# Linear attention and a GELU layer on one core: a warm-up in five fp32 matmuls, warm matmuls between the first kv and x steps, and first touches spread over rows

## The chip, the cores and the metric

The kernel runs on one core of a Trainium2 chip. The metric is the device time of one execution in microseconds. A program on one core has no second die to compare with, but each execution lists the mean clock that TensorE was granted.

## The reference, cut to what matters

```python
q_s = softmax of q over the 64 features          # batch 8, heads 8, sequence 576
k_s = softmax of k over the sequence
kv  = einsum('bhsd,bhse->bhde', k_s, v)
x   = einsum('bhsd,bhde->bhse', q_s, kv)          # as 4608 tokens x 512
out = gelu(x @ w_in) @ w_out                      # 512 -> 2048 -> 512, fp32 in and out
```

(The original spells the softmaxes out, and GELU with erf.)

## The kernel before: the parts that the change and the argument touch

TensorE works in bf16. For each batch: transposes of q, kv products, x products, then the h stage (64 matmuls of 128x512 for `x @ w_in`) and the y stage (64 for `@ w_out`). Batch 0 has no earlier batch to hide behind, so its front waits for the loads, and 27 matmuls on zeros, the warm-up, fill TensorE meanwhile (in before's trace their weight loads start 0.43 us apart until 4.07 us; at the full clock that the trace records from 3.98 on, a matmul of this shape takes 0.216, 64 of them 13.81).

```python
zeros = singles.tile([128, 512], BF16)

def warm(n):
    ps = psum_y.tile([128, DM], FP32, tag="y")
    for i in range(n):
        nc.tensor.matmul(ps, zeros[:, 0:128], zeros, start=True, stop=True)

touch = singles.tile([16, 4, 2], FP32)           # four tiny reads on another queue
for i, a in enumerate((k[0, 0, 0:16, 0:2], v[0, 0, 0:16, 0:2],
                       moe_w_in[0:16, 0:2], moe_w_out[0:16, 0:2])):
    nc.scalar.dma_start(out=touch[:, i, :], in_=a)

load_main(0, "q", q, 2); load_pair(0, "k", k, 2); load_pair(0, "v", v, 4)
wi = [load_wi(i) for i in range(5)]              # w_in in blocks of 256, 256, 512, 512, 512 columns
wo = [load_wo(i) for i in range(3)]              # ... batch 1, the last of w_out, batch 2
nc.vector.memset(zeros, 0.0)
setup_tiles()                                    # three more VectorE memsets
warm(27)
...
tp_mm(0, 0)                                      # transposes
warm(2)
...
tp_mm(0, 1)
kv_mm(0, 0); kv_norm(0, 0, 1); tp_evac(0, 1)     # kv, its normalisation on VectorE
x_mm(0, 0)                                       # x needs the normalised kv
...
kv_mm(0, 1); kv_norm(0, 1, 2); x_mm(0, 1)
h_phase(0, {0: [cast of w_in block 2], 2: [block 3], 6: [block 4], ...})

def y_last():                                    # the very end: the last tile in two pieces
    for (c0, n) in ((0, 384), (384, 128)):
        ...                                      # 16 matmuls, copy on VectorE,
        eng.dma_start(out=..., in_=y_sb)         # stores of 64 rows on two queues
```

(Condensed; calls joined on one line, `...` marks cuts. Block 2 of w_in, the third, comes in four loads of 128 rows each, each cast by VectorE. A 128-column tile takes columns from all of its block's 512, so its four contraction steps need all four casts.)

The softmax here doesn't subtract the row's maximum and nothing guards it: scores larger than these inputs give would overflow.

## Time and profile before

| | before |
|---|---|
| time, median of the first 3 executions | 283.38 us (283.36 to 284.02) |
| span of the profiled execution (its time was 283.92 us) | 282.1 us |
| mean granted clock in it | 0.991 |
| dense TensorE work begins (first h matmul) | 15.00 us |
| last matmul ends | 278.4 us |

The span is the part of the time that the profile sees; it is about 1.8 us shorter than the time. What else matters before the prediction is in the page's strips of 40 slices, each 7.05 us long: the granted clock in tenths, and what the DMA engines moved.

```profile
PEclk9979999999999999999999999999999999999998
GB/s 233 382 404 428 401 402 406 401 223 55 136 83 349 163 80 249 379 41 39 221 369 47 74 198 346 89 77 164 136 0 74 149 2 0 74 77 0 2 74 74
```

Slice 3 (14 to 21 us) has a clock of 0.7 on average, and from the second to the eighth slice the loads run at about 400 GB/s without pause. Whatever comes earlier on TensorE meets that stream.

### The profile page before, as it was taken

The numbers are of one execution on the slowest core, as the hardware profiler recorded it, in microseconds if no ns is written. First come the engines' busy times: TensorE is split into PE (matmuls) and PEld (weight loads), VectorE is DVE, ScalarE is ACT, GpSimd is POOL, SyncE is SP. The second block draws the span as 40 slices with busy tenths as digits, with TensorE's granted clock in tenths as the row PEclk, the third lists the DMA queues.
The fourth block names the chain that finished last, engine by engine and source line by source line (L and its number), as shares of the span: only waits on it lengthen the run. The fifth ranks groups of instructions, "written<-read, shape, count | busy, mean of one in ns | idle before, by whom it ended". The sixth has DMA issues, their size and how long they took to land.

```text
span 282.1 us, 4576 instructions
## 1 busy us (share of the span) xinstructions
PE 273.1 (97%) x1933; PEld 126.3 (45%) x1933; DVE 101.8 (36%) x149; ACT 156.7 (56%) x242; POOL 32.8 (12%) x25
## 2 busy tenths in 40 slices
PE   8699999999999899999999999999999999999994
PEld 3334454444444344444444444444444444444443
DVE  2766586309760470075006510562006200230021
ACT  5756753689467914693468436862683364036400
POOL 0530040002020050005000500050005000000000
PEclk9979999999999999999999999999999999999998
DMA  7999999951629429911991179226601500120033
GB/s 233 382 404 428 401 402 406 401 223 55 136 83 349 163 80 249 379 41 39 221 369 47 74 198 346 89 77 164 136 0 74 149 2 0 74 77 0 2 74 74
DMA packets 44852, 50.09 MB, mean 178 GB/s; under 512 B 20385, under 2 KB 29857, under 8 KB 44577
## 3 DMA queue, kind: packets, MB, share of 16 engines
q1 hardware_dynamic: 44544, 49.68, 51.9%
q8 instruction: 15, 0.25, 0.4%
q10 hardware_dynamic: 288, 0.13, 0.2%
q14 instruction: 5, 0.03, 0.1%
HBM read 36.70 MB, written 9.44 MB: 164 GB/s over the span
## 4 chain that ended last, share of the span: by engine, by line
PE 84%; DMA 7%; DVE 3%; ACT 2%; SPq 1%; issue 1%; POOL 0%; ACTq 0%
PE ps L294 40%; PE ps L304 39%; DMA f<-in_v_dram 6%; PE kv L165 2%; PE ps L250 2%; DMA f<-in_q_dram 1%; PE ps L326 1%; DVE v_aug L144 1%; DVE qsum L195 1%; ACT ek L137 1%; ACT e L132 1%; DVE e L197 1%; SPq L230 0%; DVE y_sb L311 0%; ACT L132 0%
## 5 line engine op out<-in xcount | busy, mean ns | idle before, releaser
L294 PE MATMUL ps<-xT,wi_bf 128*128 128x512 bf16 x576 | 127.2, 382 | 0.0
L304 PE MATMUL ps<-wo_bf,g 128*128 128x512 bf16 x560 | 124.4, 379 | 1.3 <-DVE y_sb L311 1.3
L299 ACT ACTIVATE g<-ps 128x512 bf16<-128x512 f32 x144 | 85.6, 597 | 68.6 <-PE ps L294 68.6
L294 PEld LDWEIGHTS <-wi_bf 128*128 128x128 bf16 x576 | 56.6, 99 | 69.2 <-issue 1.9
L304 PEld LDWEIGHTS <-g 128*128 128x128 bf16 x560 | 54.0, 98 | 65.7 <-issue 2.0
L311 DVE COPY y_sb<-ps 128x512 f32<-128x512 f32 x35 | 23.8, 683 | 74.5 <-PE ps L304 74.1
L197 POOL TENSOR_TENSOR e<-e,recq 128x2048 bf16<-128x2048 bf16 (+1 forms) x9 | 25.7, 2855 | 179.1 <-DVE recq L196 146.9
L144 DVE CAST v_aug<-f 128x576 bf16<-128x576 f32 x26 | 17.9, 745 | 57.3 <-DMA f<-in_v_dram 57.2
L276 ACT CAST xT<-ps 128x512 bf16<-128x512 f32 x19 | 10.2, 588 | 31.9 <-PE ps L250 22.3
L195 DVE TENSOR_REDUCE qsum<-e 128x16 f32<-128x1024 bf16 (+1 forms) x13 | 21.0, 1618 | 15.6 <-ACT e L132 15.6
L132 ACT ACTIVATE e<-f 128x512 bf16<-128x512 f32 (+1 forms) x42 | 20.5, 556 | 1.2 <-DMA f<-in_q_dram 1.1
L137 ACT ACTIVATE ek<-f 128x2304 bf16<-128x2304 f32 (+1 forms) x10 | 17.2, 1730 | 2.4 <-DMA f<-in_k_dram 2.4
L274 DVE CAST xT<-ps 128x512 bf16<-128x512 f32 x15 | 9.7, 686 | 15.5 <-PE ps L250 12.7
L78 ACT ACT_TABLE_LOAD x9 | 11.5, 1283 | 2.8 <-issue 2.6
L404 PE MATMUL ps<-zeros 128*128 128x512 bf16 x29 | 8.0, 435 | 1.2 <-DVE scr L73 1.2
L132 ACT ACT_TABLE_LOAD x7 | 9.0, 1283 | 0.1
L165 PEld LDWEIGHTS <-ek 64*64 64x64 bf16 x576 | 6.6, 105 | 3.1 <-issue 1.2
L378 DVE CAST wi_bf<-w 128x512 bf16<-128x512 f32 (+1 forms) x8 | 7.1, 903 | 2.1 <-DMA w<-in_moe_w_in_dram 2.0
L165 PE MATMUL kv<-v_aug,ek 64*64 64x65 bf16 x576 | 7.1, 193 | 0.7 <-POOL v_aug L144 0.4
L397 DVE CAST wo_bf<-w 128x2048 bf16<-128x2048 f32 (+1 forms) x5 | 5.1, 1013 | 4.5 <-DMA w<-in_moe_w_out_dram 4.4
L197 DVE TENSOR_TENSOR e<-e,recq 128x1024 bf16<-128x1024 bf16 x4 | 6.3, 1586 | 0.1
L250 PE MATMUL ps<-qT,kvc 64*64 64x512 bf16 x60 | 5.2, 406 | 1.2 <-DVE kvc L176 1.2
(29 smaller groups left out, 40.5 us busy)
## 6 DMA issues: line engine op xcount, KB each, us to landing
out_dram<-y_sb SPq DMA_DIRECT2D x32, 256.0 KB, 2.3
f<-in_k_dram SPq DMA_DIRECT2D x6, 1152.0 KB, 10.0
f<-in_v_dram SPq DMA_DIRECT2D x6, 1152.0 KB, 11.6
f<-in_q_dram SPq DMA_DIRECT2D x6, 1024.0 KB, 7.5
w<-in_moe_w_in_dram SPq DMA_DIRECT2D x6, 512.0 KB, 8.4
f<-in_k_dram SPq DMA_DIRECT2D x4, 576.0 KB, 10.1
f<-in_v_dram SPq DMA_DIRECT2D x8, 288.0 KB, 8.1
f<-in_q_dram SPq DMA_DIRECT2D x4, 512.0 KB, 8.6
```

Source lines behind the costliest of these rows:

```text
L78: nc.scalar.activation(out=scr[:, 1:2], in_=scr[:, 0:1], func=func)
L132: nc.scalar.activation(out=dst[:, i], in_=src[:, u], func=AF.Exp)
L137: nc.scalar.activation(out=ek[b % 2][:, i:i + n], in_=st[b]["kf"][:, i:i + n].rearrange("p x (n d) -> p x n d", n=NS), func=AF.Exp,)
L144: eng.tensor_copy(out=v_aug[b % 2][:, hp, :, 0:D], in_=st[b]["vf"][:, hp, :].rearrange("p (n d) -> p n d", n=NS),)
L165: nc.tensor.matmul(ps[c, i, half, 0:D + 1], ek[b % 2][pr, hp, n, :], v_aug[b % 2][pr, hp, n, 0:D + 1], start=(n == 0), stop=(n == NS - 1),)
L195: nc.vector.reduce_sum(out=qsum, in_=eq[:, :, hs, :], axis=AX.X)
L197: eng.tensor_tensor(out=eq[:, :, hs, :], in0=eq[:, :, hs, :], in1=recq.unsqueeze(3).to_broadcast([128, J, w, D]), op=ALU.mult,)
L250: nc.tensor.matmul(ps[c, :], kvc[b][pr, hp, :], st[b]["qT"][pr, :, hp, :], start=True, stop=True,)
L294: nc.tensor.matmul(ps, wi_bf[:, dm, t * 128:(t + 1) * 128], xT[:, dm, :], start=(dm == 0), stop=(dm == NDM - 1),)
L299: nc.scalar.activation(out=g[:, t, :], in_=ps, func=AF.Gelu)
L304: nc.tensor.matmul(ps, st[c]["g"][:, t, j * 128:(j + 1) * 128], wo_bf[:, t, :], start=(t == 0), stop=(t == NDF - 1),)
L311: nc.vector.tensor_copy(out=y_sb, in_=ps)
```

## The change

Its intent: spend fewer instructions on the warm-up, keep TensorE's clock from falling while it waits in the front of batch 0, and let the tiny first reads reach more of the memory that the first loads will read.

```diff
     zeros = singles.tile([128, 512], BF16)
+    zeros32 = singles.tile([128, 512], FP32)
@@
-    def warm(n):
+    def warm(n, z=zeros):
         ps = psum_y.tile([128, DM], FP32, tag="y")
         for i in range(n):
-            nc.tensor.matmul(ps, zeros[:, 0:128], zeros, start=True, stop=True)
+            nc.tensor.matmul(ps, z[:, 0:128], z, start=True, stop=True)
+
+    def warm_x():
+        for r in range(2):
+            for i in range(2):
+                pr = slice(r * 64, r * 64 + 64)
+                c = slice((r ^ i) * 64, (r ^ i) * 64 + 64)
+                nc.tensor.matmul(
+                    st[0][f"x{i}"][c, :], zeros[pr, 0:64], zeros[pr, :], start=True, stop=True,
+                )
@@
-    for i, a in enumerate((k[0, 0, 0:16, 0:2], v[0, 0, 0:16, 0:2],
-                           moe_w_in[0:16, 0:2], moe_w_out[0:16, 0:2])):
+    for i, a in enumerate((k[0].rearrange("h (p n) d -> (h p) (n d)", n=NS)[0:128:8, 0:2],
+                           v[0].rearrange("h (p n) d -> (h p) (n d)", n=NS)[0:128:8, 0:2],
+                           moe_w_in[0:128:8, 0:2], moe_w_out[0:512:32, 0:2])):
@@
+    nc.vector.memset(zeros32, 0.0)
     nc.vector.memset(zeros, 0.0)
     setup_tiles()
-    warm(27)
+    warm(5, zeros32)
@@
     tp_mm(0, 1)
+    warm(2)
     ...
     tp_evac(0, 1)
+    warm_x()
     x_mm(0, 0)
```

The two groups of warm matmuls in the last hunk are called the filler below.

## The prediction

> **What bounds the kernel now.** I read the summary of engines first, then the chain that ended last, then the timeline and half-microsecond windows of the first 22 us, because every edited line runs there.
>
> ```profile
> PE 273.1 (97%) x1933; PEld 126.3 (45%) x1933; DVE 101.8 (36%) x149; ACT 156.7 (56%) x242; POOL 32.8 (12%) x25
> ...
> PE 84%; DMA 7%; DVE 3%; ACT 2%; SPq 1%; issue 1%; POOL 0%; ACTq 0%
> ```
>
> The matmul engine is busy for 273.1 of 282.1 us and carries 84% of the chain. From 15.0 us on it has almost no gap: 0.13 us near 67, 1.32 us near 98, and the store at the end. So whatever the change does to the first 20 us moves the whole rest by the same amount, if no other wait swallows it. The later waits mostly hang on TensorE's own progress: the 1.32 us wait at 98 goes back, in the chain, through a load of v, a transpose and a normalisation to a y copy released by TensorE at 76.87. They should move along.
>
> In the first 20 us two views matter. The timeline gives the order of work:
>
> ```profile
> 1.19 7.36 PE L404 MATMUL ps<-zeros 128*128 128x512 bf16 x27 [1.19 <-DVE scr L73]
> ...
> 11.16 2.14 POOL L144 CAST v_aug<-f 128x576 bf16<-128x576 f32 x3 [1.89 <-DMA f<-in_v_dram]
> ...
> 11.88 0.47 PE L165 MATMUL kv<-v_aug,ek 64*64 64x65 bf16 x34 [0.43 <-POOL v_aug L144]
> ...
> 12.95 0.41 PE L250 MATMUL ps<-qT,kvc 64*64 64x512 bf16 x4 [0.60 <-DVE kvc L176]
> ...
> 14.42 0.64 PE L250 MATMUL ps<-qT,kvc 64*64 64x512 bf16 x4 [0.60 <-DVE kvc L176]
> ...
> 15.00 15.27 PE L294 MATMUL ps<-xT,wi_bf 128*128 128x512 bf16 x64
> ```
>
> Columns are start, duration, engine, line, work, and in brackets the idle time before it with its releaser. The front is paced by the arrival of v (11.16), then kv, normalisation, x, and finally the dense stream at 15.00. The windows (length, busy time of the engine with its number of instructions, granted clock, DMA share, GB/s), cut where the clock changes and stepped back by the same 3.41 us, show the other thing:
>
> ```profile
> 1.19:3.99 2.80, 2.80 (x7) 1.00 0.66 209
> 3.99:7.40 3.41, 3.41 (x17) 1.00 1.03 345
> 7.40:10.81 3.41, 2.51 (x22) 1.00 1.01 377
> 10.81:14.22 3.41, 1.86 (x82) 1.00 1.08 392
> 14.22:17.64 3.42, 3.22 (x11) 0.50 1.06 403
> 17.64:21.05 3.41, 3.41 (x18) 1.00 1.05 405
> ```
>
> After a window in which TensorE was busy for only 1.86 of 3.41 us, the clock is 0.50 for exactly one such window, just as the dense stream starts. After one with 2.51 us it stayed at 1.00. (The 1.00 before 3.99 is not to be believed: the warm-up's weight loads are 0.43 us apart until 4.07, and pack together only after.)
>
> [...] half clock from 14.22 to 17.64, 3.42 us, and a warm-up that speeds up at 4.0. [...] the four touches here land 1.6, 3.4, 4.4 and 5.2 us after issue[...].
>
> **The change part by part.**
>
> 1. *Warm-up.* 27 bf16 matmuls become five fp32 ones. A full-rate 128x512 bf16 pass is 13.81/64 = 0.216 us (the 64 matmuls of a later undisturbed h stage take 13.81 us in the chain); a half-rate one is 0.427 us. [...] The larger memset (512 words where 256 took 0.27 us) adds about 0.27 us, so the start goes from 1.19 to about 1.45. [...] I expect an end of 7 to 9 us against 8.55. The next work, the first transposes at 9.33, waits for POOL, so this part by itself is worth 0.0 us on the path.
>
> 2. *Filler.* Two 128x512 matmuls after the second transposes: 2 x 0.216 = 0.43 us, put into the wait for v_aug that ends at 11.88. Four 64x512 matmuls between the first kv group and x: by the x row 0.41 us, put into the 0.60 us in which TensorE waits for kvc (12.38 to 12.95). Both fit into idle time, cost at most 0.05 us, and raise the window 10.81 to 14.22 from 1.86 to about 2.70 us busy, over the 2.51 that kept the clock. So I expect the half-rate window to vanish.
>
> 3. *What that is worth.* The 64 h matmuls of batch 0 run from 15.00 to 30.11, 15.11 us, against 13.81: 1.30 us lost to the clock, plus 0.64 - 0.41 = 0.23 in the last x group. Gross gain 1.5 us. But not all arrives, because w_in is still landing. The timeline of the weight casts:
>
> ```profile
> 15.99 2.08 DVE L378 CAST wi_bf<-w 128x512 bf16<-128x512 f32 x3 [0.19 <-DMA w<-in_moe_w_in_dram]
> ...
> 18.92 0.62 DVE L378 CAST wi_bf<-w 128x512 bf16<-128x512 f32 x1 [0.85 <-DMA w<-in_moe_w_in_dram]
> ```
>
> The fourth part of the third block is cast at 19.54. It is used first by the 20th h matmul (5th column tile, last contraction). At full rate from 14.85 that one would be due at 14.85 + 19 x 0.216 = 18.95, so it waits 0.6 us. Before, with some 6.2 slow matmuls by 17.64, it was due at 17.64 + 12.8 x 0.216 = 20.4, and did not wait. The gain on that matmul is thus 20.4 - 19.6 = 0.8 us. The later blocks (last cast at 25.01) leave room: the 49th matmul would be due at 19.6 + 29 x 0.216 = 25.9. So **0.8 us of the 1.5** comes through if the loads land as before.
>
> 4. *Touches.* The four tiny reads move from the first 16 rows (for k and v, within one head) to rows spread over what the first loads cover. Same count, size and queue. If a first access to a region is slow, this takes it away from the bulk load. In the half-microsecond windows the rate from 2.5 to 8.5 us averages 349 GB/s, with dips to 288 and 265 at 5.0 to 6.0, against some 395 afterwards: a deficit of 6 x 46/395 = 0.7 us at most. A share of it, perhaps 0.15 to 0.3 us, may be recovered, and it would move v and the w_in blocks together, so it adds to the 0.8. Against it: [...] the traces of its waits show 1.0 us for the touch of w_out and 0.6 us for that of w_in. If spread touches land later, issue of the loads slips. I count +0.15 us gain.
>
> Sum: 283.38 - 0.8 - 0.15 = about 282.4 where the clock holds.
>
> **The rivals.**
>
> [...] If fp32 passes or 64-row filler count less than full bf16 matmuls, or if the shorter warm-up leaves the window 7.40 to 10.81 too thin (it lost up to 1.15 us of dense work, 2.51 to perhaps 1.4 with an end at 7.0), the clock drops at 10.81 instead, and the transposes, kv and x run at half rate; then it costs some 0.5 to 1 us on the front and the gain is gone: 283.4 to 284.4. I give this about one in four. For it: the margin is a guess from two windows. Against it: the filler is placed just where the thin window is[...].
>
> *The loads take all of it.* If more than one w_in part is late, the h stage simply waits longer and the gain shrinks to 0.3 us or less: 283.1. For it: DMA is at 390 to 424 GB/s until 22 us, with 2.0 us of vector casts waiting for w_in. Against it: only one part is due before it lands by my count.
>
> *The full gross gain.* If touches pull every load forward by 0.6 us, nothing waits and 1.5 + 0.6 comes through: 281.3. The rate deficit allows it only if all of it is first-touch cost, and the q load, which has no touch, is no faster than the rest.
>
> **Range and chances.** Three in four at about 282.4, one in four at about 283.5, mean 282.6. [...] I predict 282.6, range 281.6 to 283.8. Two per cent is 5.7 us, more than everything lost to idle and clock before 20 us that this could recover, so within 2% is near certain.
>
> **What would show it.** A clock of 1.00 in all windows from 10 to 20 us, and a first h stage of 13.8 us plus one wait of some 0.6 us near the 20th matmul released by the vector cast, confirm parts 2 and 3. A 0.50 window anywhere between 10 and 18 refutes part 2. [...] v cast starting before 10.9, and rates above 370 GB/s in 5 to 8 us, would show that the touches matter. I would be wrong if the warm-up ran past 9.3 us and held the transposes, if filler delayed x, or if an early gain were lost again at a load that doesn't follow TensorE, such as q, k and v of batch 1 (k lands 37.5, v from 40.7) or w_out's last part near 40.

The forecast's sum is 283.38 - 0.8 - 0.15 = about 282.4; with one chance in four of about 283.5 it became 282.6. The working of the warm-up's end rested on an assumed cost of an fp32 matmul: the 7 to 9 us, and the 7.0 in the first rival, are the estimate from it, and the part enters the sum with 0.0 us. The first rival is that the clock falls anyway, or earlier; what it says of fp32 and 64-row matmuls is a guess, and an argument against it, that the five fp32 matmuls fill the old length, is cut (they took 7.06 us, against 7.36 before). The waits in part 4 are those of the queue of loads: in before's trace it waited 1.0 us for the touch of w_out and 0.6 us for that of w_in. The load of q, no faster than the rest, lands mostly in the windows from 2.5 to 5.0 us, at 338 to 383 GB/s. That first accesses are slow was a guess too; the runs below don't show it (283.13 us with the spread touches alone, 283.15 without).

## The result, and the profile after

The changed kernel took 283.70 us (median of 6 executions, 283.46 to 284.08), the kernel before 283.37 (6 executions, 282.91 to 284.02). The ratio is 1.001, with a 95% interval of 0.9995 to 1.0026: the same. Ratios are the mean time of one kernel's fast runs over that of the other's of the same rounds, so not quite the ratio of the medians.

The predicted time was 282.6, with a range up to 283.8. That the number lies in the range says little: the expected gain of 0.8 to 1.0 us is not there. The profile after shows that the front did what was meant. First the summary and the chain by engine, from the page:

```profile
PE 272.0 (96%) x1922; PEld 125.8 (45%) x1922; DVE 102.1 (36%) x150; ACT 156.8 (56%) x242; POOL 32.9 (12%) x25
...
PE 81%; DMA 10%; DVE 3%; ACT 2%; SPq 1%; issue 1%; ACTq 0%
```

Then the timeline of the front, as shown of before (lines have moved by one: L405 is the warm-up, L413 the filler before x, L166 kv, L251 x, L295 h, L379 the weight casts):

```profile
1.45 7.06 PE L405 MATMUL ps<-zeros 128*128 128x512 f32 x10 [1.45 <-DVE zeros L436]
...
11.52 0.59 PE L166 MATMUL kv<-v_aug,ek 64*64 64x65 bf16 x36
...
11.92 0.41 PE L413 MATMUL ps<-zeros 64*64 64x512 bf16 x4
...
12.71 0.41 PE L251 MATMUL ps<-qT,kvc 64*64 64x512 bf16 x4 [0.38 <-DVE kvc L177]
...
14.21 0.41 PE L251 MATMUL ps<-qT,kvc 64*64 64x512 bf16 x4 [0.60 <-DVE kvc L177]
...
14.55 4.28 PE L295 MATMUL ps<-xT,wi_bf 128*128 128x512 bf16 x19
...
19.17 0.61 DVE L379 CAST wi_bf<-w 128x512 bf16<-128x512 f32 x1 [1.32 <-DMA w<-in_moe_w_in_dram]
...
19.84 2.33 PE L295 MATMUL ps<-xT,wi_bf 128*128 128x512 bf16 x10 [1.01 <-DVE wi_bf L379]
```

And the windows at the same cuts (length, busy time of TensorE, weight loads, VectorE, ScalarE and GpSimd with their instructions, clock, DMA share, GB/s):

```profile
7.40:10.81 3.41, 2.43 (x18) 1.04 (x17) 3.34 (x4) 2.49 (x3) 1.90 (x1) 1.00 1.02 389
10.81:14.22 3.41, 2.43 (x92) 1.29 (x90) 1.77 (x6) 3.29 (x5) 2.48 (x4) 1.00 1.07 390
14.22:17.64 3.42, 3.42 (x19) 1.54 (x20) 2.63 (x4) 1.96 (x5) 1.98 (x4) 1.00 1.06 405
17.64:21.05 3.41, 2.40 (x12) 0.94 (x11) 1.46 (x3) 1.50 (x3) 0.00 (x0) 1.00 1.05 404
```

The clock is 1.00 throughout; the second window has 2.43 us of work where before had 1.86. (These are before's cuts; where the windows of the clock lay in this trace is taken up in the last part.) The dense work begins at 14.55, and exactly the 20th matmul waits, 1.01 us, for the fourth cast of the third w_in block. By the first y matmul (29.57 after, 30.11 before) 0.54 us are won, and the last matmul ends at 277.65 instead of 278.39, 0.74 us earlier. Yet the spans are 282.0 and 282.1. So the gain was given back **after the last matmul**. From its end to the end of the span it is 4.35 us after, and 3.71 before. (Spans are printed to 0.1 us, so such differences are good to about 0.05.) The last stores, from the DMA view of the last few microseconds (size in KB, then time from issue to landing; q14 is the queue of instruction loads), before:

```profile
q14 instruction: 1, 0.01, 0.6%
out_dram<-y_sb SPq DMA_DIRECT2D x1, 96.0 KB, 2.1
out_dram<-y_sb ACTq DMA_DIRECT2D x1, 96.0 KB, 2.4
out_dram<-y_sb SPq DMA_DIRECT2D x1, 32.0 KB, 2.0
out_dram<-y_sb ACTq DMA_DIRECT2D x1, 32.0 KB, 2.1
```

and after:

```profile
q14 instruction: 1, 0.01, 0.3%
out_dram<-y_sb SPq DMA_DIRECT2D x1, 96.0 KB, 2.1
out_dram<-y_sb ACTq DMA_DIRECT2D x1, 96.0 KB, 2.8
out_dram<-y_sb SPq DMA_DIRECT2D x1, 32.0 KB, 2.9
out_dram<-y_sb ACTq DMA_DIRECT2D x1, 32.0 KB, 3.1
```

Three of the four last stores take 0.4 to 1.0 us longer to land. At this point that could have been chance in one trace. It was not looked at in the prediction at all.

### The profile page after: what moved, and what is told of

It is laid out like the page before. It is cut to its first block, busy times and chain, and to the rows that moved or that the text cites. A ratio compares the mean times of both kernels' runs of the same rounds, so it can differ in the third digit from the quotient of the medians.

```text
span 282.0 us, 4555 instructions
## 1 busy us (share of the span) xinstructions
PE 272.0 (96%) x1922; PEld 125.8 (45%) x1922; DVE 102.1 (36%) x150; ACT 156.8 (56%) x242; POOL 32.9 (12%) x25
## 4 chain that ended last, share of the span: by engine, by line
PE 81%; DMA 10%; DVE 3%; ACT 2%; SPq 1%; issue 1%; ACTq 0%
PE ps L305 39%; PE ps L295 38%; DMA f<-in_v_dram 6%; DMA w<-in_moe_w_in_dram 3%; PE kv L166 2%; DMA f<-in_q_dram 1%; PE ps L251 1%; PE ps L327 1%; DVE v_aug L145 1%; DVE qsum L196 1%; ACT ek L138 1%; ACT e L133 1%; DVE e L198 1%; SPq L231 0%; DVE y_sb L312 0%
## 5 line engine op out<-in xcount | busy, mean ns | idle before, releaser
L295 PE MATMUL ps<-xT,wi_bf 128*128 128x512 bf16 x576 | 126.1, 379 | 1.0 <-DVE wi_bf L379 1.0
L295 PEld LDWEIGHTS <-wi_bf 128*128 128x128 bf16 x576 | 56.2, 98 | 69.3 <-DVE wi_bf L379 1.5
L405 PE MATMUL ps<-zeros 128*128 128x512 f32 (+1 forms) x14 | 8.3, 734 | 1.5 <-DVE zeros L436 1.5
L379 DVE CAST wi_bf<-w 128x512 bf16<-128x512 f32 (+1 forms) x8 | 7.1, 909 | 2.8 <-DMA w<-in_moe_w_in_dram 2.8
L166 PEld LDWEIGHTS <-ek 64*64 64x64 bf16 x576 | 6.5, 105 | 2.9 <-issue 1.1
L166 PE MATMUL kv<-v_aug,ek 64*64 64x65 bf16 x576 | 7.1, 193 | 0.1
L251 PE MATMUL ps<-qT,kvc 64*64 64x512 bf16 x60 | 5.0, 390 | 1.0 <-DVE kvc L177 1.0
```

What stands on the lines that cost most here:

```text
L166: nc.tensor.matmul(ps[c, i, half, 0:D + 1], ek[b % 2][pr, hp, n, :], v_aug[b % 2][pr, hp, n, 0:D + 1], start=(n == 0), stop=(n == NS - 1),)
L295: nc.tensor.matmul(ps, wi_bf[:, dm, t * 128:(t + 1) * 128], xT[:, dm, :], start=(dm == 0), stop=(dm == NDM - 1),)
```

## The experiments

Twelve kernels were run. Each had six executions, with the kernel before beside them on the same chip. On three chips the full-clock executions of the kernel before average 283.09, 283.27 and 283.07 us, so pooling, as is done below, brings in 0.2 us at most. The indented texts are what was expected, written before each run. "Full clock" below means executions with a mean clock of 0.9945 or more (all of these have 0.996 or more), "half-clock" the others (0.990 to 0.994).

### The two kernels once more

No edit in either.

> The kernel before, unchanged, to see the spread of its own executions. Theory A (the cold window is in every execution of it, and its cure is eaten by late weight loads): mean clock near 0.99 in all runs, a 0.50 window just before or in the first h stage in the trace, first y matmul near 30.1 to 30.3 us, last matmul ending near 278.4. Theory C (the trace seen was of an unlucky execution, most have no cold window there): several runs show clock 0.997 or more, and those are the fast ones, near 282.9 us.

> The changed kernel, unchanged. Theory A: clock 1.00, 64 h matmuls with one wait of 0.8 to 1.2 us for the last cast of the third w_in block, y from 29.7 us, last matmul ending 0.5 to 0.8 us earlier than in the kernel before of this call; if the time is still the same as before, the difference must lie after the last matmul (the last stores landing 2.0 to 3.1 us after issue), and be different from trace to trace. Theory B (the change makes the end slower itself): the stores at the end land late in this trace as well.

Before once more: 283.54 us (282.92 to 284.09); after once more: 283.74 (282.61 to 284.12). What taught something were the single executions. Those of the kernel before fall into two groups by clock. Over the 39 executions with a clock on record, 11 were half-clock, with a mean of 284.09 us (283.75 to 284.52), and 28 were full-clock, with a mean of 283.15. The changed kernel had full clock in all 12, and a mean of 283.61.

So theory C was right in part: the trace from which the prediction was made was of the rarer, slower kind. The half-rate window costs 284.09 - 283.15 = 0.94 us where it strikes, and by the mean clock it strikes in 28% of the executions: 0.27 us on average, and 0.2 us on the median (283.28 of all, 283.07 of the full-clock ones). Both traces of the kernel before happened to be of this kind (a clock of 0.50 from 14.22 to 17.64 us in the one, of 0.52 over that stretch in the other). And theory B was right in part too: at the same full clock the changed kernel is 283.61 - 283.15 = 0.46 us slower (standard error 0.15). Its second trace again has the long end, 4.39 us after the last matmul, although its last matmul ended a microsecond earlier (276.61) than in its first trace.

That microsecond is the landing of w_in. In this second trace of the same changed kernel all four casts of the third block follow each other, and nothing waits:

```profile
14.62 9.67 PE L295 MATMUL ps<-xT,wi_bf 128*128 128x512 bf16 x43
15.77 2.71 DVE L379 CAST wi_bf<-w 128x512 bf16<-128x512 f32 x4 [0.34 <-DMA w<-in_moe_w_in_dram]
19.46 1.10 DVE L379 CAST wi_bf<-w 128x1024 bf16<-128x1024 f32 x1 [0.97 <-DMA w<-in_moe_w_in_dram]
```

The wait predicted for the 20th matmul is thus there in one trace of the changed kernel and not in the other.

### Is it the one late cast, or the block's layout?

```diff
 # no_wait: in the changed kernel; wrong result on purpose
+    cs = 2 if (i == 2 and c == 3) else c
-    nc.vector.tensor_copy(out=o[:, c:c + d], in_=w[:, c:c + d])
+    nc.vector.tensor_copy(out=o[:, c:c + d], in_=w[:, cs:cs + d])
 # split: in the changed kernel
-    wi_cols = [256, 256, 512, 512, 512]
-    wi_parts = [1, 1, 4, 2, 2]
+    wi_cols = [256, 256, 256, 256, 256, 256, 512]
+    wi_parts = [1, 1, 2, 2, 1, 1, 2]
     (w_out's second and third blocks permuted to match)
```

> The changed kernel with the fourth cast of the third w_in block fed from the third part's data, which has landed earlier (wrong result on purpose; all loads unchanged). Theory A: the 1.0 us wait of TensorE near 19.8 us vanishes or shrinks to 0.3 us or less, but the fourth block (cast up to 22.75) then holds the 35th matmul for some 0.8 us, so y starts only 0.1 to 0.4 us earlier than in the changed kernel; the loads as a whole are the limit. If only the one part was late, y starts at 28.7.

> The changed kernel with the third and fourth w_in blocks loaded and cast as two halves of 256 columns each (same bytes, same number of loads, correct result), so that a column tile needs half a block and not a whole one. Theory A: no wait of TensorE near 19.8 us, h stage 13.8 to 14.1 us, y from 28.5 to 29.0 us; then 0.0 to 0.5 us lost again where v of batch 1 lands; last matmul 0.5 to 1.0 us earlier than in the changed kernel, time 282.7 to 283.2. If the loads as a whole are the limit [...], no gain over the changed kernel.

The kernel without the wait took 283.77 us (mean 283.74), no less than the changed kernel's 283.61. In its trace the first y matmul came at 28.74, as the second reading had it ("only the one part was late"), but the mean did not follow: within the noise of six executions, about 0.2 us, the wait of that one cast is not what the changed kernel lost. The split kernel (correct) took 284.58, 1.0 us more than the changed kernel. It started y at 28.79 as hoped, but its loads fell behind: by 22 us they had moved 7.40 MB against 7.57 (the rates of the 1 us windows added up), and TensorE lost the time again at batch 1's kv and at a y copy behind late casts of v near 99 us (1.69 us there, against 1.13 in the changed kernel). The expectation of 282.7 to 283.2 failed. As far as this one trace shows, ending the first h stage earlier at the price of a slower load stream is a bad trade here.

### Which part of the change costs the 0.46 us?

```diff
 # filler_only: before, plus warm(2) after tp_mm(0, 1) and warm_x() before x_mm(0, 0)
 # touch_only: before, with the four spread touches
 # fp32_only: before, with zeros32, its memset, and warm(5, zeros32) for warm(27)
 # after_old_touch: the changed kernel, with the four old touches
```

> The kernel before with the two groups of filler matmuls alone (27 bf16 warm-up matmuls and old touches kept). So far executions of the kernel before fall in two groups: clock 0.991 to 0.992, about 284.0 us, and clock 0.997 or more, about 283.1 us; the changed kernel has clock 0.996 or more in all, yet about 283.6 us. Theory A2 (the filler cures the clock and costs nothing; what eats it is another part of the change): clock 0.996 or more in all runs, mean time about 283.1 us. Theory L (with full clock the load stream is the limit in every kernel and its landing jitter alone spreads the times; before was lucky): about 283.5 us as in the changed kernel.

> The kernel before with the spread touches alone. Theory A2 with the touches as what eats the gain (k's touch lands 2.2 us after issue and not 1.6, loads slip): runs with clock 0.997 or more take about 283.6 us, those with clock 0.991 about 284.3 us or more. If touches do nothing: 283.1 and 284.0 us as in the kernel before.

> The kernel before with the fp32 warm-up alone. If the fp32 warm-up is what eats the gain, runs of full clock take about 283.6 us; if it does nothing, 283.1 us. [...] if it leaves the window before x thinner, clock 0.992 in more than half of the runs; if it shifts nothing, in about half as in the kernel before.

> The changed kernel with the old touches. If the spread touches eat the gain: about 283.1 us, w_in's last block cast by 24.3 to 24.7 us. If not: about 283.6 us as the changed kernel, clock 0.996 or more in all runs.

| kernel | fp32 warm-up | full-clock executions | their mean, us | half-clock | end after the last matmul in the trace, us |
|---|---|---|---|---|---|
| before | no | 28 | 283.15 | 11 | 3.71 and 3.81 |
| filler_only | no | 6 | 283.18 | 0 | 3.81 |
| touch_only | no | 6 | 283.13 | 0 | 3.80 |
| fp32_only | yes | 5 | 283.54 | 1 | 4.45 |
| after_old_touch | yes | 6 | 283.69 | 0 | 4.46 |
| changed kernel | yes | 12 | 283.61 | 0 | 4.35 and 4.39 |

The last column is the printed span less the modelled end of the last matmul. It splits the kernels cleanly, and the means follow it: the fp32 warm-up costs about half a microsecond, at the other end of the program. The touches do nothing that could be seen (283.13 against 283.15), and the filler costs nothing. The medians of these kernels (283.31, 282.97, 283.64 and 283.57) alone would have been too noisy to tell.

### Why would a warm-up at the start delay the last store?

The DMA view has a row of instruction loads, q14. The kernels with the fp32 warm-up have one VectorE instruction more, the memset of `zeros32`. The packets of the trace, and ever narrower windows of the DMA view, show that the last q14 load begins at 282.45 us in before's trace, after everything. In the changed kernel's it runs from 279.56 to 279.89, amid the last stores. No other packet begins in its last 0.16 us, and from 279.88 to 280.40 the changed kernel has

```profile
q10 hardware_dynamic: 5, 0.00, 4.3%
q1 hardware_dynamic: 5, 0.00, 1.5%
```

(packets, MB, share of the 16 engines). The last store on each of these two queues has 80 packets in the trace, 64 of 512 bytes and 16 of 4, so just one sixteenth of it comes after the instruction load. Three theories were put to the test: the instruction count (F), the memory that the new tile shifts (S), the fp32 matmuls themselves (P).

```diff
 # dve_plus1: in the kernel before
     nc.vector.memset(scr, 0.0)
+    nc.vector.memset(scr[:, 1:2], 0.0)
 # after_pool_zero: in the changed kernel
-    nc.vector.memset(zeros, 0.0)
+    nc.gpsimd.memset(zeros, 0.0)
```

> The kernel before with one more VectorE instruction at the start (a second memset of two bytes' worth of work, no memory added, 27 bf16 warm-up kept). In the traces so far the time from the end of the last matmul to the end of the span is 3.7 to 3.8 us in the four kernels without the fp32 warm-up and 4.35 to 4.5 us in the six with it; in the latter a small instruction load lies amid the last stores, in the former 2.4 us later. Theory F (the one more VectorE instruction that the fp32 warm-up brings, its memset, shifts that instruction load into the last stores): tail 4.35 to 4.5 us here, full-clock runs about 283.6 us, half-clock ones about 284.6. Theory S (the new 2 KB tile moves the store buffers in memory and makes the stores slower) or theory P (the fp32 matmuls themselves): tail 3.7 to 3.8 us, 283.1 and 284.0.

> The changed kernel with the memset of the bf16 zeros moved from VectorE to GpSimd, so that VectorE has as many instructions as in the kernel before; the fp32 tile and fp32 warm-up stay. Theory F: tail 3.7 to 3.8 us, clock 0.996 or more, about 283.1 us, some 0.5 under the changed kernel. Theories S and P: tail 4.35 to 4.5 us, 283.6 us.

One VectorE memset of one column, 0.06 us long, put into the kernel before: end 4.37 us, and the last stores land as in the changed kernel:

```profile
out_dram<-y_sb SPq DMA_DIRECT2D x1, 96.0 KB, 2.1
out_dram<-y_sb ACTq DMA_DIRECT2D x1, 96.0 KB, 2.8
out_dram<-y_sb SPq DMA_DIRECT2D x1, 32.0 KB, 2.9
out_dram<-y_sb ACTq DMA_DIRECT2D x1, 32.0 KB, 3.1
```

Its three full-clock executions average 283.95 us, its three half-clock ones 284.69: 0.8 and 0.6 above those of before. Its ratio to the kernel before is 1.0039 (1.0017 to 1.0061), some of it because three of its six executions were half-clock and only three of the eleven beside it. The same number of VectorE instructions restored in the changed kernel, with the fp32 tile and the fp32 matmuls in place: end 3.71 us, and

```profile
out_dram<-y_sb SPq DMA_DIRECT2D x1, 96.0 KB, 2.1
out_dram<-y_sb ACTq DMA_DIRECT2D x1, 96.0 KB, 2.4
out_dram<-y_sb SPq DMA_DIRECT2D x1, 32.0 KB, 2.0
out_dram<-y_sb ACTq DMA_DIRECT2D x1, 32.0 KB, 2.1
```

282.88 us in the median, 282.90 in the mean. The last q14 load begins at 279.56 us in the first of these traces and at 281.18, after the stores, in the second. S and P fall: neither the tile nor the fp32 matmuls were touched. Shown is that one VectorE instruction more or less moves that load in or out of the last stores, and that the end moves with it, in all 14 traces (seven with 3.71 to 3.81, seven with 4.35 to 4.46). How it does so is to be seen packet by packet. In each of the seven traces with the long end the load begins 1.91 to 1.94 us after the last matmul and takes 0.31 to 0.35 us, five packets of each of the two queues start only when it is over, and the last store packet is done 2.63 to 2.67 us after the last matmul. In the seven others the load begins at least 4.06 us after it, no packet comes late, and the last one is done after 2.07 to 2.09. The trace does not name the engine of a packet; that one sixteenth of each store starts only after the load is read here as one of the core's 16 DMA engines having to do both, which is a reading and not shown. These late packets account for about 0.57 of the 0.64 us.

### Two more

```diff
 # less_load: after_pool_zero, and the fourth quarter of w_in's third block is not loaded
 #            (third quarter's data cast in its place; wrong result on purpose)
 # after_bf16: the changed kernel with warm(27) in bf16 and without zeros32
```

> The former kernel with the fourth quarter of the third w_in block neither loaded nor waited for (the third quarter's data are cast in its place: wrong result on purpose); 256 KB less in the load stream, about 0.65 us at 400 GB/s. Theory L (at full clock the load stream of the first 45 us is the limit): v of batch 1 lands 0.5 to 0.7 us earlier and the time falls by 0.3 to 0.7 us against the former kernel, to about 282.5 us. If TensorE's own work is the limit: no change, 283.1 us.

> The changed kernel with the old warm-up of 27 bf16 matmuls (filler and spread touches stay, no fp32 tile). Theory F: tail 3.7 to 3.8 us, clock 0.996 or more in all runs, about 283.1 us: below the kernel before, whose mean over 28 runs is 283.4, by what its half-clock runs cost it.

With 256 KB less to load, the cast of batch 1's v began at 39.40 us against 40.07, as expected, but the mean time fell only from 282.90 to 282.74 us, with a standard deviation of 0.4 in each six: neither theory is shown. Late loads cost something in some executions, as the two traces of the changed kernel show, but how much on average stays open. The changed kernel with the bf16 warm-up took 283.25 us (mean 283.19), full clock in all six, end 3.76: as theory F has it.

The version with the lowest times of the correct ones is the changed kernel with that memset on GpSimd: a mean of 282.90 us over six, against 283.41 for the kernel before over 39 and 283.61 for the changed kernel over 12. Its ratio to the kernel before in its own rounds is 0.9986, with an interval of 0.9966 to 1.0005. It is ahead of the changed kernel by what its end shows; that it beats the kernel before is likely but not shown.

## Why the prediction was right or wrong

**The range**: 283.70 us in 281.6 to 283.8. The middle was off by 1.1 us, for two reasons. That the range held is luck: its upper part stood for a clock that falls anyway, which did not happen. (The weighting is also off by a little: three quarters of 282.4 and one quarter of 283.5 are 282.7, not 282.6.)

**Part 1, the warm-up, "by itself is worth 0.0 us on the path": this step failed.** Its end was in the range, at 8.51 us (7 to 9). The trace has two records for each fp32 matmul. Their weight loads come 0.85 us apart before the clock's rise at 6.53 (2.47, 3.32, 4.17, 5.03) and 0.43 after it (6.64, 7.07, 7.50), so a whole one takes 0.86 at full rate, four times the 0.216 of a bf16 one. The working of the end led to 7.0, with the clock rising at 4.0. From the measured records, a rise at 3.98 gives the same: three of them by then, seven more of 0.43 us. The same estimate gives 8.3 for a rise at 6.53 and 7.3 for one at 4.48. In this trace the clock rose only at 6.53; in that of no_wait it rose at 4.48, and the warm-up ended at 7.49. So the 8.51 is owed to when the clock rose. Above all, the part was costed only where it stands. The extra memset it brings was priced at about 0.27 us of start and cost half a microsecond at the end. Over all kernels that are otherwise valid comparisons, full-clock executions with the extra VectorE instruction average 283.66 us (26 of them: changed, fp32_only, after_old_touch, dve_plus1), those without 283.13 (52: before, filler_only, touch_only, after_bf16, after_pool_zero): 0.53 us, with a standard error of 0.10.

**Part 2, the filler: right in what it did, less so in why.** It cured the half-rate window: of 54 executions with filler none was half-clock, of 57 without, 15 were. But busy time in a window, by which the prediction placed the filler, does not decide alone. In the first traces of the two kernels the changes of the clock on record are whole multiples of 3.413 us apart: 3.98, 14.22, 17.63 and 280.46 us in before's, 6.53 and 283.01 in the changed kernel's (the first of each is where the record of the clock begins and the weight loads draw together, the last lies after the last matmul). These steps are called the grid here. In the changed kernel's trace it rose at 6.53, so its windows don't lie at before's cuts; the four from there on have 2.40 to 2.92 us of work. And in the trace of no_wait, where the clock rose at 4.48, a window has less work than the 1.86 us after which it fell in before's, and it stayed at 1.00 (window, length, TensorE's busy time and matmuls, clock, DMA share, GB/s):

```profile
7.89:11.30 3.41, 1.81 (x20) 1.00 1.03 398
11.30:14.72 3.42, 2.25 (x86) 1.00 1.08 388
```

The work in that window was 16 transposes and four full 128x512 matmuls; in before's it was mostly kv products of 64x65. Whether that is what matters stays open. Where the grid lies may be why so few executions were hit: in the two traces of before the clock rose at 3.98 and 4.09, and the thin stretch is one window. In three traces of other kernels without filler (touch_only, fp32_only, dve_plus1) it rose at 5.60, 6.60 and 5.10, the thinnest window after that has 2.14 us, and the clock stayed at 1.00. This fits, but no run set the grid.

**Part 3, what that is worth: right in size where it strikes, wrong in how often.** "0.8 us of the 1.5" stands against 0.94 us measured between half-clock and full-clock executions, and the wait at the 20th matmul, 0.6 us expected, was 1.01 in the first trace and absent in the second. But the sum was taken off the median of before, as if each of its executions had the window. It was in 28%, so the part was worth 0.27 us on the mean. The prediction did allow some tenths between executions; it did not draw the conclusion that the one trace might not be typical, though its own run took 283.92 us, at the slow end of 283.36 to 284.02.

**Part 4, the touches: +0.15 us was not seen.** The touch of k landed 2.2 us after issue instead of 1.6, the first load of w_in was issued at 7.60 instead of 7.36, and the mean of touches alone is that of before (283.13 and 283.15 us). The sign that the prediction named, over 370 GB/s from 5 to 8 us, doesn't tell the touches apart: it was 328 and 375 in the two traces of the changed kernel, and 385 in fp32_only, with the old touches.

The sum by these terms: -0.27 from the clock, +0.53 from the end, 0.0 from the touches is +0.26 us; measured, the mean of the changed kernel less that of before is 283.61 - 283.41 = +0.20.

**The rivals.** None of the three happened as told. The clock didn't fall, and the loads took part of the gain in some executions but not all. The last sentence of the prediction feared a loss "again at a load that doesn't follow TensorE". It was a load of that kind, but of instructions, and at the end.

## What to carry to other kernels

Ask of a change that adds even one instruction what it does to the last microseconds: compare the time from the last matmul to the end of the span, which here repeated to 0.1 us while the whole time scattered by over one. And before costing a stall seen in one trace, look at whether every execution has it: group the executions by granted clock, since one trace, or the median of a few executions, does not tell what strikes a quarter of them.
